# A fused transformer block on one core: k projections by depth block, and the q weights two steps later

## The chip, the core and the metric

The kernel runs on one core of a Trainium2 chip. A core has a matrix engine (TensorE; PE in the profile, its weight loads PEld), a vector engine (VectorE, DVE), a scalar engine for functions of one argument (ScalarE, ACT), a general engine (GpSimd, POOL) and SyncE (SP), which here issues the DMAs. Each engine works through its own queue in order and waits for others through semaphores. TensorE writes its products to PSUM, which has eight banks of 128 x 512 fp32 here; DVE and ACT read them there. The metric is the time on the device in microseconds (us), median of several runs.

## The reference

One token sequence of 2048 rows and 512 columns goes through a linear-attention block and a gated feed-forward block, both behind a layer norm whose scale and shift come from a condition vector:

```python
mod = (_silu(c) @ w_mod).reshape(c.shape[0], 6, 1, -1)
sa, ca, ga, sb, cb, gb = (mod[:, 0], mod[:, 1], mod[:, 2], mod[:, 3], mod[:, 4], mod[:, 5])
h = _layernorm(x, axis=-1) * (1 + ca) + sa
x = x + ga * _A_ref(h, A_wqkv, A_wo)
h = _layernorm(x, axis=-1) * (1 + cb) + sb
x = x + gb * _B_ref(h, B_w_gate, B_w_up, B_w_down)
```

`_A_ref` has 32 heads of 16 columns: q, k, v are projections of h, phi(t) is t + 1 above zero and exp(t) below, plus 1e-6; kv is the sum over all tokens of phi(k) times v, z the sum of phi(k); the output is (phi(q) kv) / (phi(q) z + 1e-6), times wo. `_B_ref` is ((h w_gate) * (h w_up)) w_down with 1376 inner columns.

## The kernel before

Everything is fp32. A matrix product is made of three passes on numbers cut into a high and a low part: high x high, high x low, low x high (`product`, L191 to L198). A *split* is one ACT copy for the high part (L183) and one DVE subtraction for the low part (L184).

**Tiles.** The tokens are 4 chunks of 4 tiles of 128 rows, 16 token tiles in all, numbered i = 4 ch + j. The 512 columns are 4 depth blocks of 128. `Norm` holds a chunk: `stats` (two DVE operations for a tile, L225 and L226), `rstd_of` (a DVE addition at L233, then a power on POOL at L234), `nmr_of` (L237, DVE), `xhat` (the normalised tile, one ACT operation, L243), `transpose` (L250, four 128 x 128 transposes for a depth block, which needs the normalised tiles of the whole chunk) and `modulated` (L262 onward: ACT applies scale and shift to a transposed block, giving f; its high part is a DVE cast, L270, or a second ACT operation, L272; its low part a DVE subtraction, L273).

**The start.** While the inputs arrive, TensorE is kept busy by `keep_on(n)` (L143), n matmuls whose result nobody reads. Chunk 0 is normalised and transposed, the modulation vectors ca and sa are summed up on DVE (L159, L161) and turned into columns by TensorE: `mod_col` (L166) writes four columns into one bank, and `col_out` (L171) is one DVE operation that reads all four. Then the four k weights are split and the four depth blocks of chunk 0 modulated, and `product2` (L206 to L208) makes the k projections of token tiles 0 and 1 together, depth block by depth block. The projections of tiles 2 and 3 follow through `proj`, a whole tile at a time.

**The loop.** Over the 16 token tiles the kernel sums up T = xhat^T phi(k) in four banks (`t_tile`, L327 to L329, 12 matmuls for a tile), from which kv is made later with the v weights. Step i makes the projection of tile i + 2 ahead of its use; splits the normalised tile (`k_split_x`) and phi of tile i + 1 (`k_split`, kh on ACT at L318 and kl on DVE at L319); does `k_phi` of tile i + 2 (Relu at L291 and Exp at L292 on ACT, then L295 on DVE); adds to z (L310, L312); and runs `t_tile(i)`. In steps 0 and 1 of each chunk it *turns* the next chunk: `t_tile` of two column blocks, transposes of two depth blocks, their modulation, the other two column blocks. The next-but-one chunk's statistics are done in steps 2 and 3 of a chunk, followed in step 3 by rstd, nmr and the first two normalised tiles; the other two come in step 0 of the next chunk. So the turn of chunk 2 is in steps 4 and 5.

The table `q_at` says in which steps a q projection of chunk 0 is made (12 matmuls, then phi on ACT and DVE), and the table `extra` what is done at the end of a step: the splits of the q and v weights, and the loads and sums of the other modulation vectors.

Each engine's order is the order of the text (the schedule is manual). PSUM has two pools of four banks, `acc_bank` and `bank`; a bank is given out again when the last instruction that uses it has been issued in that order.

After the loop come the kv matrix, the attention output by token tiles (L614) and the feed-forward block, whose products (L838 and L914 to L916) take most of the span.

Of the kernel before, what the change touches and what calls it, by code (L numbers as in the profile page):

```python
# [8 lines left out]
F32 = mybir.dt.float32  # L9
F32R = mybir.dt.float32r  # L10
AF = mybir.ActivationFunctionType
ALU = mybir.AluOpType
AX = mybir.AxisListType

P = 128
# [7 lines left out]
def tile_adaln_block(  # L23
# [12 lines left out]
    nc = tc.nc  # L36
# [3 lines left out]
    KD = D // P  # L40
    NJ = 4
    CH = NJ * P
    NCH = S // CH
# [16 lines left out]
    consts = pool("consts", 1)  # L60
# [5 lines left out]
    def f32(ap):  # L66
        return ap.bitcast(F32)
# [3 lines left out]
    def T(p, tag, shape=(P, D), dt=F32, bufs=None):  # L71
        cnt[0] += 1
        return p.tile(list(shape), dt, tag="t" if p is tiles else tag, name=f"{tag}_{cnt[0]}", bufs=bufs)

    def B(tag, shape=(P, D), dt=F32):

        return T(tiles, tag, shape, dt)

    def acc_bank():
        return T(ps_acc, "acc")  # L80

    def bank():
        return T(ps_w, "bank")
# [6 lines left out]
    ones = consts.tile([P, P], F32, name="ones")  # L90
# [28 lines left out]
    def load_qkv(n):  # L119
        return [load(wqkv_v[k, :, n * D:(n + 1) * D], "raw") for k in range(KD)]  # L120
# [6 lines left out]
    raw_k = load_qkv(1)  # L127
    xts.append(load_x(1))
    raw_q = load_qkv(0)
    raw_v = load_qkv(2)  # L130
# [10 lines left out]
    def keep_on(n):  # L141
        for _ in range(n):
            nc.tensor.matmul(ps_idle, idle[:, :P], idle, start=True, stop=True)  # L143
# [19 lines left out]
    def mod_col(acc, ps):  # L163

        for b in range(KD):
            nc.tensor.matmul(ps[:, b:b + 1], acc[:, b * P:(b + 1) * P], ones[:, 0:1], start=True, stop=True)  # L166
        return ps

    def col_out(v, ps, add):
        t = consts.tile([P, KD], F32, name=f"col{v}")  # L170
        nc.vector.tensor_scalar(t, ps[:, :KD], add, None, op0=ALU.add)  # L171
        return t
# [9 lines left out]
    def split(src, h, l, low=None):  # L182
        nc.scalar.activation(h, src, AF.Copy)  # L183
        (low or nc.vector).tensor_tensor(l, src, f32(h), op=ALU.subtract)  # L184

    def split_raw(raw, shape=(P, D), low=None):
        h = B("w", shape, F32R)
        l = B("w", shape, F32R)
        split(raw, h[:raw.shape[0]], l[:raw.shape[0]], low)
        return h, l  # L190
# [6 lines left out]
            nc.tensor.matmul(ps, ah, bl, start=False, stop=False)  # L197
            nc.tensor.matmul(ps, al, bh, start=False, stop=i == n - 1)  # L198

    def product2(pss, pairs):  # L200

        n = len(pairs[0])
        for i in range(n):
            for ps, p in zip(pss, pairs):
                (ah, al), (bh, bl) = p[i]
                nc.tensor.matmul(ps, ah, bh, start=i == 0, stop=False)  # L206
                nc.tensor.matmul(ps, ah, bl, start=False, stop=False)
                nc.tensor.matmul(ps, al, bh, start=False, stop=i == n - 1)  # L208

    def cut(pair, a, b):  # L210
        return pair[0][:, a:b], pair[1][:, a:b]


    class Norm:
# [25 lines left out]
        def xhat(self, *js):  # L240
            for j in js:
                self.n[j] = B("n")
                nc.scalar.activation(self.n[j], self.tiles[j], AF.Identity,  # L243
                                     scale=self.rstd[:, j:j + 1], bias=self.nmr[:, j:j + 1])

        def transpose(self, *ks):
            for k in ks:
# [29 lines left out]
    NT = NCH * NJ  # L277
    norm = [Norm(xts[0])]
    wk, wq, wv = [], [], []
    kx, phk, phq, q_ps = {}, {}, {}, {}  # L280

    def proj(i, w, of=bank):

        ch, j = divmod(i, NJ)
        ps = of()
        product(ps, [(cut(norm[ch].t[k], j * P, (j + 1) * P), w[k]) for k in range(KD)])
        return ps

    def phi_a(ps, t):

        nc.scalar.activation(t, ps, AF.Relu, scale=-1.0)  # L291
        nc.scalar.activation(t, t, AF.Exp, scale=-1.0)  # L292
# [4 lines left out]
    def k_split_x(i):  # L297
        ch, j = divmod(i, NJ)
        kx[i] = [B("xh", dt=F32R), B("xl", dt=F32R)]
        split(norm[ch].n[j], *kx[i])  # L300

    def k_phi(i, ps):
        phi = B("phi")
        phi_a(ps, phi)
        phi_b(ps, phi)
        phk[i] = phi
# [8 lines left out]
    def k_split(i):  # L315
        h, l = B("kh", dt=F32R), B("kl", dt=F32R)
        phi = phk[i]
        nc.scalar.activation(h, phi, AF.Identity, bias=eps_phi)  # L318
        nc.vector.scalar_tensor_tensor(l, phi, EPS_PHI, f32(h), op0=ALU.add, op1=ALU.subtract)  # L319
        kx[i] += [h, l]  # L320

    def t_tile(i, *ks):
        xh, xl, kh, kl = kx[i]
        first, last = i == 0, i == NT - 1
        for k in ks:
            a, b = k * P, (k + 1) * P
            nc.tensor.matmul(tacc[k], xh[:, a:b], kh, start=first, stop=False)  # L327
            nc.tensor.matmul(tacc[k], xl[:, a:b], kh, start=False, stop=False)  # L328
            nc.tensor.matmul(tacc[k], xh[:, a:b], kl, start=False, stop=last)  # L329
# [11 lines left out]
    n0 = norm[0]  # L341
    acc_ca, acc_sa = B("f"), B("f")
# [20 lines left out]
    mod_acc(acc_sa, raw_sa, [0, 1, 2, 3])  # L363
    ca = col_out(1, ps_ca, 1.0)
    keep_on(4)
    ps_sa = mod_col(acc_sa, acc_bank())
    keep_on(9)
    wk.append(split_raw(raw_k[0]))
    sa = col_out(0, ps_sa, 0.0)
    nx = Norm(xts[1])  # L370
    nx.stats(0)
    n0.modulated(ca, sa, 0, cast=nc.vector)
    wk.append(split_raw(raw_k[1]))
    n0.modulated(ca, sa, 1, cast=nc.vector)
    wk.append(split_raw(raw_k[2]))
    n0.modulated(ca, sa, 2)
    nx.stats(1)
    wk.append(split_raw(raw_k[3]))
    n0.modulated(ca, sa, 3)
    ps0, ps1 = acc_bank(), acc_bank()  # L380
    product2((ps0, ps1), [[(cut(n0.t[k], j * P, (j + 1) * P), wk[k]) for k in range(KD)] for j in range(2)])
    nx.stats(2, 3)
    nx.rstd_of()
    k_split_x(0)
    k_phi(0, ps0)
    nx.nmr_of()
    k_phi(1, ps1)
    k_split(0)
    nx.xhat(0, 1)

    tacc = [acc_bank() for _ in range(KD)]
    rows, cols = {}, {}
# [4 lines left out]
    def mod_load(*vs):  # L397
        raw_m.update({v: load_mod(v) for v in vs})

    def mod_part(v, *ks):  # L400
        if 0 in ks:
            accs[v] = B("f")
        mod_acc(accs[v], raw_m[v], ks)

    extra = {0: lambda: (wq.extend(split_raw(r) for r in raw_q[0:1]),),
             1: lambda: (wq.extend(split_raw(r) for r in raw_q[1:2]),),
             2: lambda: (wq.extend(split_raw(r) for r in raw_q[2:4]),),
             4: lambda: (wv.extend(split_raw(r) for r in raw_v[0:1]),),
             5: lambda: (wv.extend(split_raw(r) for r in raw_v[1:2]),),
             6: lambda: (wv.extend(split_raw(r) for r in raw_v[2:3]), mod_load(2),),  # L410
             7: lambda: (wv.extend(split_raw(r) for r in raw_v[3:4]),),
             8: lambda: (mod_part(2, 0, 1), mod_load(3)),
             9: lambda: (mod_part(2, 2, 3), mod_load(4)),
# [2 lines left out]
             12: lambda: (raw_o.extend(load(wo_v[k], "raw") for k in range(KD)), mod_part(4, 2, 3), cols.update({3: col_out(3, mod_col(accs[3], bank()), 0.0)})),  # L416
             13: lambda: (mod_part(5, 0, 1, 2), cols.update({4: col_out(4, mod_col(accs[4], bank()), 1.0)})),
             14: lambda: (mod_part(5, 3), wo_s.extend(split_raw(x) for x in raw_o)), 15: lambda: rows.update({5: mod_row(5, accs[5])})}
    q_at = {3: 0, 4: 1, 6: 2, 7: 3}
    ahead = {2: proj(2, wk)}  # L420
    for i in range(NT):
        ch, j = divmod(i, NJ)
        more = ch + 1 < NCH
        if i == 0:
            ahead[3] = proj(3, wk)
        elif i > 1:
            ahead[i + 2] = proj(i + 2, wk) if i + 2 < NT else proj(i + 6 - NT, wq)
        if i in q_at:
            qps = proj(q_at[i], wq)
        if more and j == 0:  # L430
            nx.xhat(2)
        if i + 1 < NT:
            k_split_x(i + 1)
        if more and j == 0:
            nx.xhat(3)
        if i + 1 < NT:
            k_split(i + 1)
        if more and j < 2:
            t_tile(i, 0, 1)
            nx.transpose(2 * j, 2 * j + 1)  # L440
            nx.modulated(ca, sa, 2 * j, 2 * j + 1, cast=nc.vector)
            norm[ch + 1:] = [nx]
        if ch + 2 < NCH and j == 2:
            nx2 = Norm(xts[ch + 2])
            nx2.stats(0, 1)
        if ch + 2 < NCH and j == 3:
            nx = nx2
            nx.stats(2, 3)
            nx.rstd_of()
            nx.nmr_of()  # L450
            nx.xhat(0, 1)
        if i + 2 < NT:
            k_phi(i + 2, ahead.pop(i + 2))
        else:
            q_a(i + 6 - NT, ahead.pop(i + 2))
            q_b(i + 6 - NT)
        if i in q_at:
            q_a(q_at[i], qps)
            q_b(q_at[i])
        if i + 1 < NT:  # L460
            z_add(i + 1)
        if i == NT - 1:
            zps = bank()
            nc.tensor.matmul(zps, ones, zacc, start=True, stop=True)
            zb = consts.tile([P, D], F32, name="zb")
            nc.scalar.activation(zb, zps, AF.Identity, bias=eps_z)
        t_tile(i, *range(2 if more and j < 2 else 0, KD))
        if i in extra:
            extra[i]()
    ga, gb, sb, cb = rows[2], rows[5], cols[3], cols[4]  # L470
# [60 lines left out]
    ps = proj(6, wq)  # L531
# [12 lines left out]
    for g in range(KD):  # L544
        a, b = g * P, (g + 1) * P
# [4 lines left out]
    ps = proj(8, wq)  # L550
# [9 lines left out]
    ps = proj(9, wq)  # L560
# [460 lines left out]
    ps = proj(11, wq)  # L1021
# [176 lines left out]
```

## Time and profile before

| | |
|---|---|
| median of 3 runs | 569.85 us (569.65 to 570.39) |
| the profiled execution, its time | 570.02 us |
| its span in the profile | 568.3 us |
| instructions | 7356 |
| DVE, ACT, POOL busy | 373.1, 279.8, 186.2 us |
| moved by DMA | 59.34 MB |

The span runs from the first to the last recorded instruction; the execution's time is a little longer. A row of the time line gives the start, the duration, the engine, the line and operation, the output and input tiles, and in brackets how long the engine had been idle before it and what released it. Rows joined to one ("x8") give the first start and the stretch up to the last end. An instruction's listed duration can reach past the start of the next on its engine, since their parts overlap; where work follows work, the distance from start to start tells what an instruction costs. For TensorE this distance is best read from the weight loads (PEld), one before each matmul. DVE's 9 tenths of busy time in a slice mean that it has hardly a gap there; these stretches lie in the first tenth of the span:

```text
DVE  7876868868768876759767777745554434344445
ACT  3785857546456546445865545534333333334110
```

### The profile page before, as it was taken

To read this page: it belongs to the slowest core of one execution; us is meant where nothing else is said; L and a number is where in the kernel's file an instruction comes from. 1 tells how busy PE (TensorE), PEld (TensorE's weight loads), DVE (VectorE), ACT (ScalarE), POOL (GpSimd) and SP (SyncE) were. 2 spreads that over 40 slices of the span, in tenths; PEclk is the share of its full clock that TensorE was granted. 3 is DMA by queue.
4 is the path that set the end of the run, shared out by engine and by line. 5 is a ranking of instruction groups with operands and counts; after the bars stand their busy time and mean duration, and the time that the engine had idled before them with its cause. 6 is when DMAs were issued, how large, how long until landed. Compare 5 with 4: busy or idle time off the path is not lost.

```text
span 568.3 us, 7356 instructions
## 1 busy us (share of the span) xinstructions
PE 560.3 (99%) x2575; PEld 458.8 (81%) x2575; DVE 373.1 (66%) x614; ACT 279.8 (49%) x500; POOL 186.2 (33%) x191
## 2 busy tenths in 40 slices
PE   8999999999999999999989999999999999999997
PEld 6778888888888878878878888787888888888886
DVE  7876868868768876759767777745554434344445
ACT  3785857546456546445865545534333333334110
POOL 2000000000011300000579666665667446556200
PEclk9999999999999999999999999999999999999999
DMA  8900223302301000804208553599336012200004
GB/s 289 374 3 2 74 75 110 114 0 62 93 0 47 29 1 37 260 0 149 57 2 277 180 190 104 202 348 330 115 111 178 26 57 55 57 19 2 0 1 148
DMA packets 50309, 59.34 MB, mean 104 GB/s; under 512 B 6432, under 2 KB 27168, under 8 KB 50272
## 3 DMA queue, kind: packets, MB, share of 16 engines
q1 hardware_dynamic: 50272, 58.87, 32.1%
q8 instruction: 20, 0.33, 0.2%
q14 instruction: 17, 0.14, 0.1%
HBM read 43.12 MB, written 15.73 MB: 104 GB/s over the span
## 4 chain that ended last, share of the span: by engine, by line
PE 89%; DMA 3%; issue 2%; POOL 1%; DVE 1%; ACT 1%; SPq 1%; POOLq 0%; ACTq 0%
PE bank L838 28%; PE acc L914 6%; PE acc L915 6%; PE acc L916 6%; PE acc L614 6%; PE bank L198 5%; PE bank L196 5%; PE bank L197 5%; PE acc L329 3%; PE acc L327 3%; PE acc L328 3%; PE bank L693 2%; PE bank L691 2%; PE bank L692 2%; PE bank L250 2%
## 5 line engine op out<-in xcount | busy, mean ns | idle before, releaser
L838 PE MATMUL bank<-h,w 128*128 128x512 f32 (+1 forms) x798 | 185.5, 390 | 1.8 <-ACT bank L843 1.2
L838 PEld LDWEIGHTS bank<-h,w 128*128 128x128 f32 (+1 forms) x798 | 148.2, 186 | 35.3 <-ACT bank L843 1.7
L843 ACT ACTIVATE bank<-bank 128x512 f32<-128x512 f32 (+1 forms) x38 | 22.1, 583 | 144.8 <-PE bank L838 144.8
L678 DVE TENSOR_TENSOR x<-acc,x 128x512 f32<-128x512 f32 (+1 forms) x73 | 49.1, 684 | 49.0 <-PE acc L916 48.2
L824 POOL TENSOR_TENSOR w<-raw,w 128x256 fp32r<-128x256 f32 (+3 forms) x38 | 42.4, 1117 | 106.4 <-ACT w L817 86.4
L184 POOL TENSOR_TENSOR w<-raw,w 128x512 fp32r<-128x512 f32 (+1 forms) x25 | 34.9, 1399 | 116.0 <-DVE mv L226 87.6
L914 PE MATMUL acc<-w,kh 128*128 128x512 f32 (+2 forms) x154 | 59.6, 387 | 0.0
L915 PE MATMUL acc<-w,kh 128*128 128x512 f32 (+2 forms) x154 | 59.6, 387 | 0.0
L916 PE MATMUL acc<-w,kl 128*128 128x512 f32 (+2 forms) x154 | 59.5, 386 | 0.0
L234 POOL TENSOR_TENSOR rstd<-ve,half 128x4 f32<-128x4 f32 (+1 forms) x9 | 9.4, 1044 | 126.0 <-DVE ve L233 124.5
L184 DVE TENSOR_TENSOR kl<-u,kh 128x512 fp32r<-128x512 f32 (+1 forms) x38 | 26.8, 746 | 33.1 <-ACT kh L183 31.2
L824 POOL TENSOR_TENSOR w<-t,w 128x512 fp32r<-128x512 f32 (+1 forms) x38 | 48.4, 1293 | 0.0
L196 PE MATMUL bank<-w,h 128*128 128x512 f32 x112 | 45.0, 402 | 0.0
L198 PE MATMUL bank<-w,h 128*128 128x512 f32 x112 | 43.9, 392 | 0.0
L197 PE MATMUL bank<-w,h 128*128 128x512 f32 x112 | 43.6, 389 | 0.0
L614 PE MATMUL acc<-w,xh 128*128 128x512 f32 x120 | 38.1, 399 | 0.0
L914 PEld LDWEIGHTS acc<-w,kh 128*128 128x128 f32 (+1 forms) x154 | 28.9, 188 | 6.0
L916 PEld LDWEIGHTS acc<-w,kl 128*128 128x128 f32 (+1 forms) x154 | 28.9, 188 | 5.9
L915 PEld LDWEIGHTS acc<-w,kh 128*128 128x128 f32 (+1 forms) x154 | 28.9, 188 | 5.9
L893 DVE TENSOR_TENSOR u<-bank,u 128x512 f32<-128x512 f32 (+1 forms) x19 | 13.1, 690 | 30.0 <-PE bank L838 30.0
L243 ACT ACTIVATE n<-x,nmr,rstd 128x512 f32<-128x512 f32 x32 | 24.1, 804 | 17.2 <-DVE nmr L237 15.9
L262 ACT ACTIVATE f<-bank,col,col 128x512 f32<-128x512 f32 x28 | 20.7, 775 | 14.5 <-PE bank L250 12.4
(177 smaller groups left out, 1105.1 us busy)
## 6 DMA issues: line engine op xcount, KB each, us to landing
raw<-in_w_mod_dram SPq DMA_DIRECT2D x24, 256.0 KB, 3.7
raw<-in_B_w_down_dram SPq DMA_DIRECT2D x20, 256.0 KB, 2.9
raw<-in_B_w_gate_dram SPq DMA_DIRECT2D x36, 128.0 KB, 3.7
raw<-in_B_w_up_dram SPq DMA_DIRECT2D x36, 128.0 KB, 3.6
x<-in_A_x_dram SPq DMA_DIRECT2D x16, 256.0 KB, 5.4
kept<-f SPq DMA_DIRECT2D x16, 256.0 KB, 2.0
f<-kept SPq DMA_DIRECT2D x16, 256.0 KB, 4.8
side_s<-h SPq DMA_DIRECT2D x16, 256.0 KB, 2.6
```

What stands on the lines that cost most here:

```text
L184: (low or nc.vector).tensor_tensor(l, src, f32(h), op=ALU.subtract)
L196: nc.tensor.matmul(ps, ah, bh, start=i == 0, stop=False)
L197: nc.tensor.matmul(ps, ah, bl, start=False, stop=False)
L198: nc.tensor.matmul(ps, al, bh, start=False, stop=i == n - 1)
L243: nc.scalar.activation(self.n[j], self.tiles[j], AF.Identity, scale=self.rstd[:, j:j + 1], bias=self.nmr[:, j:j + 1])
L614: nc.tensor.matmul(yps[i], x, y, start=False, stop=k == KD - 1 and x is al, skip_group_check=True)
L678: nc.vector.tensor_tensor(xt[:, a:b], dn[j][:, a:b], xt[:, a:b], op=ALU.add)
L824: sub = lambda out, x, y: (on or nc.gpsimd).tensor_tensor(out, x, f32(y), op=ALU.subtract)
L838: mm = lambda x, y, **kw: nc.tensor.matmul(ps, x[:, k], y, skip_group_check=True, **kw)
L914: nc.tensor.matmul(ps, hh[:, a:b], dh[:n, c:d], start=i == 0, stop=False)
L915: nc.tensor.matmul(ps, hh[:, a:b], dl[:n, c:d], start=False, stop=False)
L916: nc.tensor.matmul(ps, hl[:, a:b], dh[:n, c:d], start=False, stop=i == len(hs) - 1)
```

## The change

Four things are changed, all of them in the first 100 us.

- The sa columns: the first is written into a bank of its own and read alone (`sa_out(0)`); the three others share a second bank and are read one by one behind block 0. Nine `keep_on` matmuls behind them become two.
- The k projections of tiles 0 to 3 are made depth block by depth block for all four tiles (`k_block`), in four banks; for blocks 2 and 3 the order is by tile. `product2` goes. All four blocks of chunk 0 take their high part by a DVE cast (before, blocks 2 and 3 took it from ACT).
- Chunk 1 is normalised in halves: statistics, rstd and nmr for its tiles 0 and 1, then statistics and rstd for tiles 2 and 3, which DVE normalises itself (`xhat_on`). Its turn moves from steps 0 and 1 to steps 1 and 2; in step 2 it stands ahead of `t_tile(2)`, and that ahead of the projection of tile 4.
- The splits of the q weights move from steps 0, 1, 2 to steps 2, 3, 4, the q projections from steps 3, 4, 6, 7 to steps 5, 6, 7, 8, and the splits of the v weights from 4, 5, 6, 7 to 5, 6, 7.

```diff
+        def xhat_on(self, engine, *js):
+            for j in js:
+                self.n[j] = B("n")
+                engine.tensor_scalar(self.n[j], self.tiles[j], self.mv[:, j, 0:1], self.rstd[:, j:j + 1],
+                                     op0=ALU.subtract, op1=ALU.mult)
...
-    ps_sa = mod_col(acc_sa, acc_bank())
-    keep_on(9)
-    wk.append(split_raw(raw_k[0]))
-    sa = col_out(0, ps_sa, 0.0)
+    ps_sa = [acc_bank()]
+    ps_sa += [acc_bank()] * (KD - 1)
+    sa = consts.tile([P, KD], F32, name="col0")
+
+    def sa_block(b):
+        nc.tensor.matmul(ps_sa[b][:, b:b + 1], acc_sa[:, b * P:(b + 1) * P], ones[:, 0:1], start=True, stop=True)
+
+    def sa_out(b):
+        nc.vector.tensor_scalar(sa[:, b:b + 1], ps_sa[b][:, b:b + 1], 0.0, None, op0=ALU.add)
+
+    def block_in(b):
+        n0.modulated(ca, sa, b, cast=nc.vector)
+
+    def w_in(b):
+        wk.append(split_raw(raw_k[b]))
+
+    for b in range(KD):
+        sa_block(b)
+    keep_on(2)
+    k_ps = [acc_bank(), acc_bank(), bank(), bank()]
+
+    def k_block(b, *js):
+        for j in js:
+            (hh, hl), (wh, wl) = cut(n0.t[b], j * P, (j + 1) * P), wk[b]
+            nc.tensor.matmul(k_ps[j], hh, wh, start=b == 0, stop=False)
+            nc.tensor.matmul(k_ps[j], hh, wl, start=False, stop=False)
+            nc.tensor.matmul(k_ps[j], hl, wh, start=False, stop=b == KD - 1)
+
+    sa_out(0)
+    w_in(0)
+    block_in(0)
+    for b in range(1, KD):
+        sa_out(b)
+    w_in(1)
+    block_in(1)
+    k_block(0, 0, 1, 2, 3)
     nx = Norm(xts[1])
+    w_in(2)
+    block_in(2)
     nx.stats(0)
-    n0.modulated(ca, sa, 0, cast=nc.vector)
-    wk.append(split_raw(raw_k[1]))
-    n0.modulated(ca, sa, 1, cast=nc.vector)
-    wk.append(split_raw(raw_k[2]))
-    n0.modulated(ca, sa, 2)
+    k_block(1, 0, 1, 2, 3)
+    w_in(3)
+    block_in(3)
     nx.stats(1)
-    wk.append(split_raw(raw_k[3]))
-    n0.modulated(ca, sa, 3)
-    ps0, ps1 = acc_bank(), acc_bank()
-    product2((ps0, ps1), [[(cut(n0.t[k], j * P, (j + 1) * P), wk[k]) for k in range(KD)] for j in range(2)])
+    nx.rstd_of(0, 2)
+    k_split_x(0)
+    k_block(2, 0)
+    k_block(3, 0)
+    k_phi(0, k_ps[0])
+    nx.nmr_of(0, 2)
+    nx.xhat(0, 1)
     nx.stats(2, 3)
-    nx.rstd_of()
-    k_split_x(0)
-    k_phi(0, ps0)
-    nx.nmr_of()
-    k_phi(1, ps1)
+    nx.rstd_of(2, 4)
     k_split(0)
-    nx.xhat(0, 1)
+    k_block(2, 1)
+    k_block(3, 1)
+    k_split_x(1)
+    k_phi(1, k_ps[1])
+    nx.xhat_on(nc.vector, 2)
+    k_split(1)
+    nx.xhat_on(nc.vector, 3)
+    k_block(2, 2)
+    k_block(3, 2)
+    k_block(2, 3)
+    k_block(3, 3)
...
-    extra = {0: lambda: (wq.extend(split_raw(r) for r in raw_q[0:1]),),
-             1: lambda: (wq.extend(split_raw(r) for r in raw_q[1:2]),),
-             2: lambda: (wq.extend(split_raw(r) for r in raw_q[2:4]),),
-             4: lambda: (wv.extend(split_raw(r) for r in raw_v[0:1]),),
-             5: lambda: (wv.extend(split_raw(r) for r in raw_v[1:2]),),
-             6: lambda: (wv.extend(split_raw(r) for r in raw_v[2:3]), mod_load(2),),
+    extra = {2: lambda: (wq.extend(split_raw(r) for r in raw_q[0:1]),),
+             3: lambda: (wq.extend(split_raw(r) for r in raw_q[1:2]),),
+             4: lambda: (wq.extend(split_raw(r) for r in raw_q[2:4]),),
+             5: lambda: (wv.extend(split_raw(r) for r in raw_v[0:1]),),
+             6: lambda: (wv.extend(split_raw(r) for r in raw_v[1:3]), mod_load(2),),
              7: lambda: (wv.extend(split_raw(r) for r in raw_v[3:4]),),
...
-    q_at = {3: 0, 4: 1, 6: 2, 7: 3}
-    ahead = {2: proj(2, wk)}
+    q_at = {5: 0, 6: 1, 7: 2, 8: 3}
+    ahead = {2: k_ps[2], 3: k_ps[3]}
+    turn_at = {4 * ch + j: (ch + 1, 2 * j, 2 * j + 1) for ch in range(1, NCH - 1) for j in range(2)}
+    turn_at.update({1: (1, 0, 1), 2: (1, 2, 3)})
     for i in range(NT):
         ch, j = divmod(i, NJ)
-        more = ch + 1 < NCH
-        if i == 0:
-            ahead[3] = proj(3, wk)
-        elif i > 1:
+        done = 0
+        if i > 2:
             ahead[i + 2] = proj(i + 2, wk) if i + 2 < NT else proj(i + 6 - NT, wq)
         if i in q_at:
             qps = proj(q_at[i], wq)
-        if more and j == 0:
+        def turn_x():
+            to, *ks = turn_at[i]
+            nx.transpose(*ks)
+            nx.modulated(ca, sa, *ks, cast=nc.vector)
+            norm[to:] = [nx]
+
+        fresh = i > 0 and ch + 1 < NCH and j == 0
+        if i == 2:
+            turn_x()
+        if fresh:
             nx.xhat(2)
-        if i + 1 < NT:
+        if 0 < i < NT - 1:
             k_split_x(i + 1)
-        if more and j == 0:
+        if fresh:
             nx.xhat(3)
-        if i + 1 < NT:
+        if 0 < i < NT - 1:
             k_split(i + 1)
-        if more and j < 2:
+        if i in turn_at and i != 2:
             t_tile(i, 0, 1)
-            nx.transpose(2 * j, 2 * j + 1)
-            nx.modulated(ca, sa, 2 * j, 2 * j + 1, cast=nc.vector)
-            norm[ch + 1:] = [nx]
+            done = 2
+            turn_x()
+        if i == 2:
+            t_tile(i, *range(KD))
+            done = KD
+            ahead[i + 2] = proj(i + 2, wk)
...
-        t_tile(i, *range(2 if more and j < 2 else 0, KD))
+        t_tile(i, *range(done, KD))
```

More of the change, by code (lines that the diff above doesn't have):

```diff
@@ L198, in product @@
             nc.tensor.matmul(ps, al, bh, start=False, stop=i == n - 1)
[L200 to L208, printed above, removed]
     def cut(pair, a, b):
```

## The prediction

> **What bounds the kernel now.** I read the page first, then the list of what the weight loads waited for, then the time lines of PE, DVE and ACT over the first 60 us, since the change ends there.
>
> ```profile
> span 568.3 us, 7356 instructions
> ...
> PE 560.3 (99%) x2575; PEld 458.8 (81%) x2575; DVE 373.1 (66%) x614; ACT 279.8 (49%) x500; POOL 186.2 (33%) x191
> ```
>
> ```profile
> PEld bank L838 <- ACT bank L843: 1.7, 1, 1.7
> ...
> PEld acc L208 <- DVE h L273: 0.8, 2, 0.4
> PEld bank L198 <- DVE h L273: 0.7, 2, 0.4
> ```
>
> TensorE is busy for 99% of the span, and once products run its waits are small: the longest is 1.7 us. The number of products is not changed. So the time moves only by how early the useful stream starts and by waits put into it or taken out, and what is gained or lost up to the point where both orders have issued the same products is carried to the end.
>
> ```profile
> 14.94 0.97 PEld L166 LDWEIGHTS acc<-ones,f 128*128 128x128 f32 x8 [0.33 <-DVE f L161]
> 15.82 1.94 PEld L143 LDWEIGHTS acc<-w 128*128 128x128 f32 x9
> 16.03 0.16 DVE L171 TENSOR_SCALAR col<-acc 128x4 f32<-128x4 f32 x1 [0.47 <-PE acc L166]
> 16.23 0.78 ACT L262 ACTIVATE f<-bank,col,col 128x512 f32<-128x512 f32 x1 [1.96 <-DVE col L171]
> 17.80 0.19 PEld L206 LDWEIGHTS acc<-w,h 128*128 128x128 f32 x1
> 18.34 0.19 PEld L208 LDWEIGHTS acc<-w,h 128*128 128x128 f32 x1
> 23.23 0.50 PE L208 MATMUL acc<-w,h 128*128 128x512 f32 x1
> 23.76 0.60 ACT L291 ACTIVATE phi<-acc 128x512 f32<-128x512 f32 x1 [1.33 <-PE acc L208]
> 24.93 0.58 ACT L291 ACTIVATE phi<-acc 128x512 f32<-128x512 f32 x1
> 29.49 0.19 PEld L327 LDWEIGHTS acc<-kh,xh 128*128 128x128 f32 x1
> 34.66 0.68 DVE L295 SCALAR_TENSOR_TENSOR phi<-bank,phi 128x512 f32<-128x512 f32 x1
> 35.26 0.68 DVE L310 TENSOR_TENSOR z<-phi,phi 128x512 f32<-128x512 f32 x1
> ...
> 42.81 0.19 PEld L196 LDWEIGHTS bank<-w,h 128*128 128x128 f32 x1
> 49.73 0.17 DVE L233 TENSOR_SCALAR ve<-mv 128x4 f32<-128x4 f32 x1
> 51.12 0.16 DVE L237 SCALAR_TENSOR_TENSOR nmr<-mv,rstd 128x4 f32<-128x4 f32 x1 [1.21 <-POOL rstd L234]
> 53.88 0.58 ACT L291 ACTIVATE h<-bank 128x512 f32<-128x512 f32 x1
> 55.03 0.80 ACT L243 ACTIVATE n<-x,nmr,rstd 128x512 f32<-128x512 f32 x1
> 56.26 0.80 ACT L243 ACTIVATE n<-x,nmr,rstd 128x512 f32<-128x512 f32 x1
> 57.77 1.03 PEld L250 LDWEIGHTS bank<-ident,n 128*128 128x128 f32 x8
> ```
>
> These rows are merged in order of time; left is the start, then the duration. Two places matter. At the start, the one DVE read of the four sa columns waits for all eight passes of L166 (16.03), and products begin at 17.80, behind nine idle-filling matmuls of L143. Later, at i=4, the transposes of chunk 2 load at 57.77, 0.71 us after the last normalised tile that they read (56.26 + 0.80 = 57.06). That slack is small, and it is there because TensorE has the q products of tiles 0 and 1 to do at i=3 and i=4.
>
> **Units.** From the load at 42.81 (product of tile 5) to 57.77 TensorE issues 66 matmuls: four projections, t_tile(3) and half of t_tile(4). One takes 14.96/66 = 0.227 us. DVE starts a tensor operation 0.60 us after the one before (34.66 to 35.26), though each is listed with 0.68. The other steps follow, from start to start, and first eight transposes from the chain of waits:
>
> ```profile
> 58.16 0.87 PE bank L250 x8
> ```
>
> ```profile
> 28.97 0.62 ACT L183 ACTIVATE xh<-n 128x512 fp32r<-128x512 f32 x1
> 29.49 0.80 ACT L243 ACTIVATE n<-x,nmr,rstd 128x512 f32<-128x512 f32 x1
> 30.20 0.71 ACT L318 ACTIVATE kh<-phi,eps_phi 128x512 fp32r<-128x512 f32 x1
> ...
> 33.60 0.42 DVE L270 CAST h<-f 128x512 fp32r<-128x512 f32 x1
> 34.05 0.69 DVE L273 TENSOR_TENSOR h<-f,h 128x512 fp32r<-128x512 f32 x1
> ...
> 42.80 0.69 DVE L225 BATCH_NORM_STATS2 st<-x 128x6 f32<-128x512 f32 x1
> ...
> 43.62 0.66 DVE L225 BATCH_NORM_STATS2 st<-x 128x6 f32<-128x512 f32 x1
> ```
>
> Copy 0.52 and normalise 0.71 on ACT; cast 0.45 and statistics with their aggregation 0.82 on DVE. One phi (Relu, Exp) is 24.93 - 23.76 = 1.17 on ACT.
>
> **The first column.** With a bank of its own it is ready after two of eight passes: 6 x 0.97/8 = 0.73 us earlier, read at 15.30, and ACT's block 0 starts at 15.50 instead of 16.23 and ends 16.28. DVE does the low part of the first k weight at 15.40 (before, it lay in the wait for the columns), the cast at 16.32, the low half from 16.77 to 17.46. Seven idle-filling matmuls go at no cost: the two that stay end near 16.3, ahead of the cast. The third matmul of the first product loads at 17.51, against 18.34: 0.8 us earlier. The other three reads (0.1 us each) stand on DVE behind block 0, and ACT's block 1 behind them, at 17.8; no matmul waits for that.
>
> **Four token tiles per block.** A block now feeds 12 matmuls, 2.7 us, where DVE needs 0.60 + 0.45 + 0.60 = 1.65 us for a weight and a block, new casts included, or 2.47 with a statistics. So the two waits at L208 shrink to one of 0.3: DVE, without a gap from 19.05 on, ends block 3's low half at 23.9. But tile 0 is finished behind 30 matmuls instead of 21: the stream, counted back from the third matmul, starts at 17.05; the last load would be at 17.05 + 29 x 0.227 = 23.65 and waits until 23.9. With 0.5 us of drain (23.23) the first phi starts at 24.45, where it started at 23.76. The 18 matmuls of the other tiles run to 28.2; before, the same 48 were done at 29.49: 1.3 us ahead here.
>
> **The first t_tiles.** TensorE now goes straight to t_tile(0), which needs kh and kl of tile 0. ACT does in its order: phi to 25.7; two normalisations at 26.6 and 27.3 (they follow nmr, which follows phi's DVE half, 25.8 + 0.6); kh from 28.0 to 28.7. TensorE waits from 28.2 to 28.75, and 0.27 more for kl (to 29.45). Tile 1 goes on in the same way: copy 28.6, phi 29.15, DVE half 30.5, kh 31.2 to 31.9. That adds 0.1 at the bank of t_tile(0)'s last column block and 0.35 at t_tile(1). New waits in sum: 1.25 us. They buy out the two at L198 (0.7): with t_tile(2) ahead of it, tile 4's product finds chunk 1's blocks ready. It ends at 42.15 by this chain (t_tile(0) ends at 31.9, then 36 matmuls, the 0.35, and two sets of eight transposes at 0.9). The same products were done at 42.81: **0.65 us gained so far**.
>
> The two tiles normalised on VectorE have no row of their form. The nearest are the modulation's operation below and the tensor operation of 0.68:
>
> ```profile
> 12.04 0.48 DVE L159 TENSOR_SCALAR f<-raw,sc 128x512 f32<-128x512 f32 x1
> ```
>
> I take 0.5, the row nearest in form. Both fall into gaps in which DVE waits for kh or phi (0.4 to 0.5 us each), so by the other end it is 0.2 us more at most. The second rstd falls into POOL's idle time.
>
> **The q weights later.** This decides. No DMA is moved (the raw q weights are loaded at the start, and the next loads stay at i=6), but the q products leave i=3, 4, 6, 7 for 5 to 8. TensorE then reaches chunk 2's transposes after proj(5), t_tile(3), proj(6) and half of t_tile(4): 42 x 0.227 = 9.55 us after 42.15, at 51.7. Of the 6.05 us by which this is earlier than 57.77, 5.45 are the two q products.
>
> Are the tiles there? DVE's half of tile 2's phi starts at 33.1 (kh of tile 1 leaves ACT at 31.8, then 1.27 of phi), against 34.66. From it to the end of the statistics DVE has 17 tensor operations, 4 casts and 4 statistics, each with its input there in time: 17 x 0.60 + 4 x 0.45 + 4 x 0.82 = 15.3, so ve comes at 48.45. (By this count the order before, with 18, 2 and 4, takes 15.0; the rows show 49.73 - 34.66 = 15.07.) The rstd takes 51.12 - 49.73 = 1.39: nmr at 49.85. Then ACT took 57.06 - 51.12 = 5.94 to the last tile; a q phi goes out of it (55.03 - 53.88 = 1.15) and the copy of the second q weight comes in (0.52): 5.3. The last tile is there at 55.2. **TensorE waits 3.5 us**, and all its later products, the q products too, are queued behind these transposes.
>
> **Sum.** A gain of 0.65 and a wait of 3.5 make +2.9 (or: 55.25 for the transposes, plus 5.45 of products still owed, less 57.77). Later turns give nothing back: at i=8 all four q products lie ahead of chunk 3's transposes, as they did, and TensorE stays the bound. The profiled execution took 570.02 us, with a span of 568.3, so this one would take 572.9; the median of the runs is 0.17 lower, hence **572.8 us**.
>
> **Rivals.** (a) *DVE closes its gaps.* My chain has 2.6 us of DVE waits between 15 and 33 us, for blocks (0.3, 0.3), phi (0.5, 0.5) and kh (0.5, 0.4, 0.1). With none, ve is at 45.85, the transposes at 52.6, the sum 0.3: 570.1. Against it: all of these inputs come from ACT in a fixed order. (b) *The turn is not late*: if nmr is there by 46.4 (51.7 - 5.3), i=4 has no wait and the gain of 0.65 stays, 569.2; with the kh waits gone too it is 1.9, 567.9. For it speaks that ACT idles in places, against it that DVE's work alone ends later. (c) *The first column is not earlier*, if its read still waits for all passes: 0.73 more, 573.5. (d) *The wait slows TensorE behind it.*
>
> ```profile
> 6.00 1.97 PEld L143 LDWEIGHTS acc<-w 128*128 128x128 f32 x5
> ...
> 292.18 2.59 PEld L838 LDWEIGHTS bank<-h,w 128*128 128x128 f32 x12 [1.66 <-ACT bank L843]
> ```
>
> At the start of the run matmuls go every 0.4 us until about 8 us. If 3.5 us without work bring this back for as long, 15 matmuls lose 0.17 each: +2.6, 575.4. After 1.66 us of waiting (292.18) twelve loads take 0.22 each, so that wait did not.
>
> [...]
>
> **How the numbers follow.** Forecast 0.70, (a) 0.09, (b) 0.07, (c) 0.06, (d) 0.08. A measurement here tells some 0.2%, 1.1 us, from no change, so same is 568.7 to 571.0. Slower is the forecast, (c) and (d), less 0.04 for a wait that falls far short: 0.80. Same is (a), that 0.04 and a little of (b): 0.14; faster is the rest, 0.06. The range goes from (a), 570.1, to just inside (d), 575.0.
>
> **What would show it.** Right: a wait of 3 to 4 us at L250 near 51.7 us, released by ACT's n; the first phi at 24.5; short waits at L327 to L329 near 28 us. Wrong: no wait over 1 us at L250 between 45 and 60 us, or ve before 46.5, or DVE work with gaps between 33 and 48 us, which would be a wait that my chain misses.

## The result

| | before | change |
|---|---|---|
| median | 570.18 us (6 runs, 569.65 to 570.82) | 573.02 us (6 runs, 571.59 to 574.66) |
| ratio to before | | 1.0048, 95% interval 1.0037 to 1.0060 |
| the profiled execution's span | 568.3 us | 572.9 us |
| its mean granted clock | 0.999 | 0.994 |

The change makes the kernel 2.8 us slower; 2.9 were forecast. The profiled execution, at 574.66, is the slowest of the six, and its page shows something that the page of before doesn't have:

```profile
span 572.9 us, 7349 instructions
...
PE 561.2 (98%) x2568; PEld 458.9 (80%) x2568; DVE 375.3 (66%) x622; ACT 276.7 (48%) x496; POOL 186.3 (33%) x192
...
PEclk9998899999999999999999999999999999999999
```

In the clock's row the fourth and fifth slices (43 to 72 us) are below full. The list of waits of the weight loads names the new waits (total, times, longest):

```profile
PEld bank L246 <- ACT n L233: 3.2, 2, 2.1
...
PEld acc L323 <- ACT kh L314: 0.9, 2, 0.6
PEld acc L325 <- DVE kl L315: 0.9, 2, 0.4
```

L246 is the line of the chunk transposes (L250 before); L323 and L325 are `t_tile` (L327, L329). No product L198 stands in the list any more. Rows chosen from the time lines of PEld, ACT and DVE of the changed kernel, merged, from the start to the late turn:

```profile
12.15 2.33 DVE L161 SCALAR_TENSOR_TENSOR f<-raw,sc,f 128x512 f32<-128x512 f32 x3
14.96 0.16 DVE L370 TENSOR_SCALAR col<-acc 128x1 f32<-128x1 f32 x1 [0.40 <-PE acc L367]
17.17 0.19 PEld L388 LDWEIGHTS acc<-w,h 128*128 128x128 f32 x1 [0.36 <-DVE h L269]
23.92 0.60 ACT L287 ACTIVATE phi<-acc 128x512 f32<-128x512 f32 x1 [3.02 <-PE acc L388]
28.20 0.19 PEld L323 LDWEIGHTS acc<-kh,xh 128*128 128x128 f32 x1 [0.65 <-ACT kh L314]
28.93 0.19 PEld L325 LDWEIGHTS acc<-kl,xh 128*128 128x128 f32 x1 [0.43 <-DVE kl L315]
...
41.48 0.19 PEld L196 LDWEIGHTS bank<-w,h 128*128 128x128 f32 x1
47.95 0.17 DVE L223 TENSOR_SCALAR ve<-mv 128x4 f32<-128x4 f32 x1
49.33 0.16 DVE L227 SCALAR_TENSOR_TENSOR nmr<-mv,rstd 128x4 f32<-128x4 f32 x1 [1.21 <-POOL rstd L224]
51.00 0.37 PEld L246 LDWEIGHTS bank<-ident,n 128*128 128x128 f32 x2
53.47 0.14 PEld L246 LDWEIGHTS bank<-ident,n 128*128 128x128 f32 x1 [2.09 <-ACT n L233]
53.84 0.80 ACT L233 ACTIVATE n<-x,nmr,rstd 128x512 f32<-128x512 f32 x1
54.69 0.93 PEld L246 LDWEIGHTS bank<-ident,n 128*128 128x128 f32 x5 [1.09 <-ACT n L233]
55.60 0.34 PEld L323 LDWEIGHTS acc<-kh,xh 128*128 128x128 f32 x1
```

Two rows of the kernel before, for comparison:

```profile
12.56 2.33 DVE L161 SCALAR_TENSOR_TENSOR f<-raw,sc,f 128x512 f32<-128x512 f32 x3
58.76 0.19 PEld L327 LDWEIGHTS acc<-kh,xh 128*128 128x128 f32 x1
```

The input data came 0.41 us earlier in this execution than in that of before: the sum over sa ends at 12.15 + 2.33 = 14.48, against 12.56 + 2.33 = 14.89 there. All that follows is shifted by it, so it is taken off in what is said of steps. TensorE is at the transposes at 51.0, does those of the first two tiles, waits 2.09 us for the third tile and 1.09 for the fourth. The second half of `t_tile(4)` loads at 55.60. Before, it loaded right behind the transposes, at 58.76. With the 5.45 us of q products still owed and the shift of 0.41, the turn is 55.60 + 5.45 + 0.41 - 58.76 = 2.7 us late.

What comes behind is the second loss. The stages of the changed kernel: start and end, length, then the busy time and instructions of PE, PEld, DVE, ACT and POOL, and at the end granted clock, DMA share and GB/s:

```profile
50.00:52.00 2.00, 1.61 (x9) 1.09 (x7) 0.00 (x0) 1.97 (x4) 0.00 (x0) 1.00 0.00 0
52.00:54.00 2.00, 0.33 (x1) 0.14 (x1) 1.78 (x3) 2.00 (x5) 0.00 (x0) 0.99 0.00 0
54.00:56.00 2.00, 1.31 (x6) 1.31 (x7) 1.41 (x3) 1.98 (x3) 0.00 (x0) 0.50 0.00 0
56.00:58.00 2.00, 2.00 (x7) 1.52 (x6) 1.84 (x4) 1.91 (x4) 0.00 (x0) 0.50 0.00 0
58.00:60.00 2.00, 2.00 (x6) 1.60 (x5) 2.00 (x4) 2.00 (x4) 0.00 (x0) 0.50 0.20 31
60.00:62.00 2.00, 2.00 (x8) 1.59 (x7) 1.91 (x4) 0.16 (x1) 0.00 (x0) 0.81 0.94 307
```

Between 54 and 60 us TensorE runs at half its clock (0.50 in these three stages). Its loads then follow each other by 0.43 us, and it does 13 matmuls from 55.60 to 60.88, which at 0.227 take 2.95 us: 2.3 us lost. So the spans' difference of 4.6 is made up: -0.41 from the data, +2.7 from the turn, +2.3 from the clock. Some 0.4 of the 2.7 is the clock as well: the last five transposes take 0.93 us here, and 0.53 in e2_q_late_alone below, where it was still full.

The low stretch here lasts from 53.96, by the mean of 0.99 in the 52 to 54 stage, to 60.76, by the 0.81 in the last one: some 6.8 us. In three other traces below (e1, e2, e5) it is half of that, 3.4 us: e5's stages stand below, e2's of 2 us from 54 on have means of 0.98, 0.50 and 0.66, and e1's of 4 us from 8 on 0.99 and 0.59. The clock fell within the second of the two waits, when the loads had waited 2.4 us in sum (2.09 and, from 53.61 on, 0.35). In e2 and e5 it fell 0.65 and 0.4 us behind the second wait, with 2.4 and 3.2 us waited in sum; in e1, 1.5 us behind a single wait of 2.6. Behind a wait of 2.21 us in e6's trace it stayed at 1.00. What sets the moment of the fall and the length of the low stretch isn't shown.

### The profile page after: what moved, and what is told of

It reads as the page before. It is cut to its first block, busy times and chain, and to the rows that moved or that the text cites. A ratio compares the mean times of both kernels' runs of the same rounds, so it can differ in the third digit from the quotient of the medians.

```text
span 572.9 us, 7349 instructions
## 1 busy us (share of the span) xinstructions
PE 561.2 (98%) x2568; PEld 458.9 (80%) x2568; DVE 375.3 (66%) x622; ACT 276.7 (48%) x496; POOL 186.3 (33%) x192
## 4 chain that ended last, share of the span: by engine, by line
PE 85%; DVE 4%; ACT 4%; issue 2%; DMA 2%; POOL 2%; SPq 0%; POOLq 0%; DVEq 0%
PE bank L886 27%; PE acc L963 6%; PE acc L962 6%; PE acc L964 6%; PE acc L662 6%; PE bank L196 4%; PE bank L197 4%; PE bank L198 4%; PE bank L741 2%; PE bank L739 2%; PE bank L740 2%; PE acc L325 2%; PE acc L323 2%; PE acc L324 2%; PE bank L246 2%
## 5 line engine op out<-in xcount | busy, mean ns | idle before, releaser
L184 DVE TENSOR_TENSOR kl<-u,kh 128x512 fp32r<-128x512 f32 (+1 forms) x38 | 27.3, 757 | 33.1 <-ACT kh L183 31.2
L196 PE MATMUL bank<-w,h 128*128 128x512 f32 x104 | 42.2, 406 | 0.0
L197 PE MATMUL bank<-w,h 128*128 128x512 f32 x104 | 41.0, 394 | 0.0
L198 PE MATMUL bank<-w,h 128*128 128x512 f32 x104 | 40.9, 394 | 0.0
L233 ACT ACTIVATE n<-x,nmr,rstd 128x512 f32<-128x512 f32 x30 | 22.6, 804 | 17.8 <-DVE nmr L227 17.8
```

## The experiments

All ratios are against the kernel before on the same chip. e1 to e4 ran on one chip, where its median was 570.87 us; e5 to e8 and then e9 and e10 ran on another, where it was 570.65 and 570.48. Where the text says that a run was at full clock, its mean granted clock was 0.999 or 1.000. The kernel before was below that in 4 of its 76 runs, all in the last group.

**e1_q_back: the q tables of before in the changed kernel.** (The splits of the v weights, in the lines left out, go back with them.)

```diff
-    extra = {2: lambda: (wq.extend(split_raw(r) for r in raw_q[0:1]),),
-             3: lambda: (wq.extend(split_raw(r) for r in raw_q[1:2]),),
-             4: lambda: (wq.extend(split_raw(r) for r in raw_q[2:4]),),
+    extra = {0: lambda: (wq.extend(split_raw(r) for r in raw_q[0:1]),),
+             1: lambda: (wq.extend(split_raw(r) for r in raw_q[1:2]),),
+             2: lambda: (wq.extend(split_raw(r) for r in raw_q[2:4]),),
...
-    q_at = {5: 0, 6: 1, 7: 2, 8: 3}
+    q_at = {3: 0, 4: 1, 6: 2, 7: 3}
```

> The change with the two tables of the q weights as before: splits at the end of steps 0, 1, 2, q projections in steps 3, 4, 6, 7. Theory (the q products are what covered the making of chunk 2's normalised tiles): no wait above 0.3 us at the transposes of chunk 2; the other parts come to -0.1 to -0.6 us, so 569.6 to 570.1. Rival (the loss comes from the new order of the start, the late first phi and the waits at the first t_tiles): it stays above 571.5.

Measured: 569.31 us, ratio 0.9975 (0.9966 to 0.9985). The wait at chunk 2's transposes is gone: they load as eight, without an idle time in front.

```profile
43.88 0.19 PEld L198 LDWEIGHTS bank<-w,h 128*128 128x128 f32 x1 [0.43 <-DVE h L269]
48.48 0.19 PEld L197 LDWEIGHTS bank<-w,h 128*128 128x128 f32 x1 [0.17 <-DVE w L184]
59.04 1.02 PEld L246 LDWEIGHTS bank<-ident,n 128*128 128x128 f32 x8
```

So the q tables turn a gain into a loss, and the other three parts of the change are a gain: 1.4 us, more than the 0.1 to 0.6 that I had expected. The trace that was kept is of the slowest of the twelve runs, 571.17 us, the only one below full clock. There the clock fell at the start, behind a wait of 2.6 us for the first chunk's tiles, and not at chunk 2's turn (a stage, then two rows of the time line):

```profile
12.00:14.00 2.00, 2.00 (x9) 1.52 (x8) 1.93 (x4) 0.51 (x1) 0.00 (x0) 0.50 1.04 384
...
12.93 2.33 DVE L161 SCALAR_TENSOR_TENSOR f<-raw,sc,f 128x512 f32<-128x512 f32 x3
17.17 0.16 DVE L370 TENSOR_SCALAR col<-acc 128x1 f32<-128x1 f32 x1 [0.99 <-PE acc L367]
```

The first column is read 17.17 - 15.26 = 1.91 us behind the sum over sa, where the changed kernel's trace has 14.96 - 14.48 = 0.48. Without these 1.43 us chunk 2's transposes come 59.04 - 15.26 - 1.43 = 42.35 us behind the sum, against 57.77 - 14.89 = 42.88 before. By this estimate 0.5 us are gained up to there, as expected; where the other 0.9 come from stays open.

**e2_q_late_alone: only the q tables, in the kernel before** (the same edit the other way round).

> The kernel before with only the two tables of the q weights of the change. Theory: ve comes 1.8 us earlier (three splits fewer ahead of it on DVE), TensorE 5.45 + 0.8 us earlier, so it waits some 2.5 us at chunk 2's transposes and the sum is +2.0 to +2.3 us: 572.2 to 572.5 where the clock holds, up to 2.6 us more in runs in which it halves behind the wait. Rival (start order): no change, 569.9 to 570.5.

Measured: 572.61 us, ratio 1.0034 (1.0022 to 1.0046), +1.9 us. At full clock (four of eight runs) the median is 572.06, just below the 572.2 to 572.5 expected, but only 1.2 over this chip's median of before, less than the 2.4 us of waits in its trace; why, stays open. The late turn comes from the tables alone, with no part of the new start: the loads of the transposes wait in the same two pieces.

```profile
54.04 0.14 PEld L250 LDWEIGHTS bank<-ident,n 128*128 128x128 f32 x1 [1.32 <-ACT n L243]
55.27 0.53 PEld L250 LDWEIGHTS bank<-ident,n 128*128 128x128 f32 x5 [1.09 <-ACT n L243]
```

**e3_fill_wait: 14 idle-filling matmuls ahead of the late transposes.**

```diff
-            nx.transpose(*ks)
+            nx.transpose(*ks, fill=14 if i == 4 else 0)
...
                 ps = turn_bank[0]()
+                for _ in range(fill if k == ks[0] else 0):
+                    nc.tensor.matmul(ps, idle[:, :P], idle, start=True, stop=True)
```

> The change with 14 idle-filling matmuls into the bank of the first transposes at step 4, ahead of them: 14 x 0.227 = 3.2 us, inside the wait. Theory (the halved clock behind the wait is a cost of its own, present in some runs): granted clock 1.00 in every run, times within 1.2 us of each other as those of before are, median 571.4 to 572.4. Rival (the clock costs nothing, the wait is all): as the change, 573.0 with a scatter of 3 us.

Measured: 571.92 us, ratio 1.0025 (1.0016 to 1.0034). The stages of its trace:

```profile
50.00:55.00 5.00, 5.00 (x26) 4.09 (x25) 2.49 (x4) 4.97 (x9) 0.00 (x0) 1.00 0.00 0
55.00:60.00 5.00, 5.00 (x26) 4.25 (x26) 4.43 (x8) 4.97 (x9) 0.00 (x0) 1.00 0.36 113
```

TensorE is kept busy through the wait and the clock stays at 1.00. Ten of its twelve runs are at full clock, with a median of 571.87; the two others (0.997 and 0.996; 573.10 and 572.80) have no trace, and where their clock fell isn't known. On the same chip e1 has 569.30 in its runs at full clock, so the late turn by itself costs 2.6 us. The changed kernel without the fill was not run on this chip.

**e5_change_again: the changed kernel once more.**

> The changed kernel itself, on the chip of the next three runs. Theory (a late turn of 2.0 to 2.7 us, and a halved clock behind it in part of the runs): 2.0 to 2.9 us over before in the median, runs with granted clock 0.999 or 1.000 near +2.0, runs with 0.994 to 0.997 up to 2.6 us above those. Rival (the scatter is not tied to the clock): times do not fall with the clock.

Measured: 573.06 us, ratio 1.0038 (1.0025 to 1.0050). One of the five runs has a clock of 0.999, with 571.47 us; the other four (0.996, 0.997) take 572.72 to 573.50, median 573.08, 1.6 more. This time the low stretch is half as long, as the stages show:

```profile
54.00:56.00 2.00, 1.10 (x7) 0.97 (x7) 1.43 (x3) 2.00 (x4) 0.00 (x0) 0.85 0.00 0
56.00:58.00 2.00, 2.00 (x7) 1.52 (x6) 1.86 (x5) 1.97 (x5) 0.00 (x0) 0.50 0.00 0
58.00:60.00 2.00, 2.00 (x9) 1.60 (x8) 2.00 (x4) 2.00 (x5) 0.00 (x0) 0.80 0.18 30
60.00:62.00 2.00, 2.00 (x10) 1.67 (x9) 2.00 (x4) 0.24 (x1) 0.00 (x0) 1.00 0.96 313
```

Together with the six runs of the result, 8 of 11 runs of the changed kernel have a clock below 0.998. In e2, where the wait is shorter, it is 4 of 8, and their median is 573.23 against 572.06 for the others. A run's mean doesn't tell where in it the clock fell: the traces of the result, of e5 and of e2 have it at chunk 2's turn, that of e1 at the start.

**e6_tiles_ahead: the last two tiles of chunk 2 normalised at once with the first two.**

```diff
-        fresh = i > 0 and ch + 1 < NCH and j == 0
+        fresh = i > 4 and ch + 1 < NCH and j == 0
...
-            nx.xhat(0, 1)
+            nx.xhat(*(range(NJ) if i == 3 else (0, 1)))
```

> The change, with the last two normalised tiles of chunk 2 made on ACT right behind the first two, in step 3: ahead of one phi (1.17), one weight copy (0.52) and one tile copy (0.52). Theory (the chain on ACT behind nmr sets the wait): the wait at chunk 2's transposes falls by 2.2 us to about 1, and the time by 2.2 us or more against the change, so between -0.3 and +0.7 us to before; the clock stays at 1.000. Rival (what counts is when DVE ends the statistics, or the displaced phi is late in turn): it gains less than 1 us on the change.

Measured: 571.60 us, ratio 1.0025 (1.0015 to 1.0036). That is 1.5 us less than the change's median in e5 (573.06), between the 2.2 of the theory and the rival's 1, and it comes mostly from the clock: 9 of its 12 runs are at full clock, with a median of 571.37, and the change's one such run in e5 has 571.47. The waits at the transposes did fall by 2.2 us, from 3.2 to 1.0:

```profile
51.80 0.14 PEld L246 LDWEIGHTS bank<-ident,n 128*128 128x128 f32 x1 [0.43 <-ACT n L233]
52.51 0.53 PEld L246 LDWEIGHTS bank<-ident,n 128*128 128x128 f32 x5 [0.57 <-ACT n L233]
...
60.79 0.19 PEld L197 LDWEIGHTS bank<-w,h 128*128 128x128 f32 x1 [2.21 <-DVE w L184]
```

The chain on ACT was named rightly, and the 2.2 us were lost again 8 us later: the first q product, now reached sooner, waits 2.21 us for the low part of a q weight, whose split the change had moved to the end of step 4. The two tables make two things late, and only the first had shown.

**e4_column_alone: the first column's bank, in the kernel before.**

```diff
-    ps_sa = mod_col(acc_sa, acc_bank())
-    keep_on(9)
-    wk.append(split_raw(raw_k[0]))
-    sa = col_out(0, ps_sa, 0.0)
-    nx = Norm(xts[1])
-    nx.stats(0)
-    n0.modulated(ca, sa, 0, cast=nc.vector)
+    ps_sa = [acc_bank()]
+    ps_sa += [acc_bank()] * (KD - 1)
...
+    keep_on(2)
...
+    sa_out(0)
+    wk.append(split_raw(raw_k[0]))
+    n0.modulated(ca, sa, 0, cast=nc.vector)
+    for b in range(1, KD):
+        sa_out(b)
+    nx = Norm(xts[1])
+    nx.stats(0)
```

> The kernel before with only the first sa column in a bank of its own, two idle-filling matmuls behind it, and the statistics of the next chunk's first tile behind block 0. The prediction's step taken alone: products start 0.7 us earlier and the end is 0.7 us earlier, 569.4. Rival (with two token tiles for a block VectorE sets the pace, and its work of this stretch has only lost the cover of the column's wait): block 1 is late by 1.0 to 1.2 us on TensorE, and the end is where it was or 0.3 us later, 570.0 to 570.6.

Measured: 570.48 us, ratio 0.9995 (0.9985 to 1.0004): no change to be seen. The products start earlier and the second block is late, as the rival had it:

```profile
17.05 0.19 PEld L206 LDWEIGHTS acc<-w,h 128*128 128x128 f32 x1 [0.78 <-PE acc L143]
17.71 0.19 PEld L208 LDWEIGHTS acc<-w,h 128*128 128x128 f32 x1 [0.37 <-DVE h L273]
19.65 0.19 PEld L206 LDWEIGHTS acc<-w,h 128*128 128x128 f32 x1 [1.18 <-DVE h L270]
```

With two token tiles for a block TensorE needs 1.4 us a block, less than VectorE's 1.65. So the earlier column is worth nothing with two tiles; that it is worth something with four is argued, since no run takes it out of the change. (The stretches in which DVE is 9 tenths busy do not lie in the first tenth of the span, as the section on the profile says: its row has 7, 8, 7 and 6 there. That VectorE is the limit here is read from these waits for it.)

**e9_stats_behind: the statistics of chunk 1's first tile behind block 1, in the kernel before.**

```diff
-    nx = Norm(xts[1])
-    nx.stats(0)
     n0.modulated(ca, sa, 0, cast=nc.vector)
     wk.append(split_raw(raw_k[1]))
     n0.modulated(ca, sa, 1, cast=nc.vector)
+    nx = Norm(xts[1])
+    nx.stats(0)
```

> The kernel before with the statistics of chunk 1's first tile moved on VectorE from ahead of block 0's cast to behind block 1. Theory (on this machine they often wait for that tile's DMA, 0.85 us in one trace, and hold up block 0): 0.4 to 0.8 us less than before. Rival (VectorE's list of work is the bound, and a place in it is worth nothing): within 0.3 us of before.

Measured: 570.62 us, ratio 1.0001 (0.9992 to 1.0010). The theory fell: on this chip the order before has such a wait too (0.64 us in e8's trace), the trace of e9 doesn't, and nothing is gained. That makes it unlikely that the 0.85 us of e2's trace are what e1 gained beyond the expectation; on the chip of e1 and e2 the move was not run.

**e8_before_pool and e7_q_back_pool: the low parts of the q weights and of the fourth k weight on GpSimd,** in the kernel before and in e1.

```diff
-    wk.append(split_raw(raw_k[3]))
+    wk.append(split_raw(raw_k[3], low=nc.gpsimd))
...
-    extra = {0: lambda: (wq.extend(split_raw(r) for r in raw_q[0:1]),),
+    extra = {0: lambda: (wq.extend(split_raw(r, low=nc.gpsimd) for r in raw_q[0:1]),),
```

> The kernel before with the low parts of the four q weights and of the fourth k weight on GpSimd, nothing else. Theory (VectorE's list of work sets the products' waits in the first 40 us): the waits at L198 (0.7) and one at L208 (0.4) and L207 (0.2) go, -0.9 to -1.3 us to before. Rival (as above): no change.

> The change with the q tables of before, and the low parts of the four q weights and of the fourth k weight on GpSimd (1.4 us each there, idle then) in place of VectorE (0.6 each). Theory (VectorE's list of work sets the blocks of chunk 1 and of block 3): the waits left at L198 and L388 go (0.3 + 0.2 + 0.2 us), so 0.5 to 0.8 us less than with the q tables alone, 1.9 to 2.3 us less than before. Rival (GpSimd slows VectorE, or its rstd is late): no gain over the q tables alone, -1.4.

Measured: e8 571.89 us, ratio 1.0017 (1.0008 to 1.0026); e7 570.30 us, 0.9993 (0.9984 to 1.0002). By the ratios both are about 1 us slower than without the move (e7 against e1's 0.9975, each on its own chip). Rows of e8, POOL and DVE merged:

```profile
35.64 0.68 DVE L295 SCALAR_TENSOR_TENSOR phi<-bank,phi 128x512 f32<-128x512 f32 x1
35.89 1.29 POOL L184 TENSOR_TENSOR w<-raw,w 128x512 fp32r<-128x512 f32 x1 [8.45 <-ACT w L183]
36.24 1.49 DVE L310 TENSOR_TENSOR z<-phi,phi 128x512 f32<-128x512 f32 x1
37.66 0.68 DVE L184 TENSOR_TENSOR xl<-n,xh 128x512 fp32r<-128x512 f32 x1
...
40.17 1.31 POOL L184 TENSOR_TENSOR w<-raw,w 128x512 fp32r<-128x512 f32 x1 [2.98 <-ACT w L183]
40.37 1.65 DVE L273 TENSOR_TENSOR h<-f,h 128x512 fp32r<-128x512 f32 x1
```

Each subtraction on GpSimd takes its 0.60 us off DVE, but the DVE operation with both inputs in SBUF that begins while it runs lasts 1.49 or 1.65 instead of 0.68. The one with an input in PSUM (35.64) runs on undisturbed, with 0.68. The first ends at 36.24 + 1.49 = 37.73, 0.55 after GpSimd's end at 37.18. So it is with five such operations in the traces of e8 and e7: they last 1.49 to 1.79 us and end 0.54 to 0.56 after GpSimd, not much less than the 0.60 that one costs by itself. That looks as if each waited for GpSimd's end; no row shows the wait itself.

**e10_start_reordered: e1, with ACT's order between the first phi and the first t_tiles changed.** The edit changes VectorE's order too: nmr and the subtraction for tile 1's normalised x go ahead of the first phi, and kl of tile 0 ahead of the second rstd's addition.

```diff
     k_split_x(0)
     k_block(2, 0)
     k_block(3, 0)
+    k_split_x(1)
+    nx.nmr_of(0, 2)
+    k_block(2, 1)
+    k_block(3, 1)
     k_phi(0, k_ps[0])
-    nx.nmr_of(0, 2)
-    nx.xhat(0, 1)
+    nx.xhat(0)
     nx.stats(2, 3)
-    nx.rstd_of(2, 4)
     k_split(0)
-    k_block(2, 1)
-    k_block(3, 1)
-    k_split_x(1)
+    nx.rstd_of(2, 4)
     k_phi(1, k_ps[1])
+    nx.xhat(1)
     nx.xhat_on(nc.vector, 2)
     k_split(1)
-    nx.xhat_on(nc.vector, 3)
...
+    nx.xhat_on(nc.vector, 3)
```

> The change with the q tables of before, and ACT's order between the first phi and the first t_tiles changed: one normalised tile of chunk 1, kh of tile 0, the phi of tile 1, then the other normalised tile (before: both, then kh and the phi); the copy of tile 1's normalised x and the nmr go ahead of the first phi. Theory (kh of tile 0 and the phi of tile 1 set the waits at the first t_tiles): the waits at L323 and L325 near 28 to 33 us, 1.25 us in sum, shrink to 0.3, and the time is 2.0 to 2.6 us under before. Rival (the waits only move to the transposes of chunk 1 or to tile 4's product): as with the q tables alone, -1.0 to -1.9.

Measured: **567.37 us** (5 runs, 567.13 to 567.93), ratio 0.9941 (0.9927 to 0.9955), all five with a clock of 0.999 or 1.000. This version beats both kernels, before by 3.1 us, more than the 2.0 to 2.6 of the theory. Between the products of block 3 and the turn of chunk 2 one wait is left, and no product L198 waits:

```profile
28.82 0.19 PEld L325 LDWEIGHTS acc<-kl,xh 128*128 128x128 f32 x1 [0.50 <-DVE kl L315]
32.35 1.03 PEld L246 LDWEIGHTS bank<-ident,n 128*128 128x128 f32 x8
34.61 1.03 PEld L246 LDWEIGHTS bank<-ident,n 128*128 128x128 f32 x8
55.92 1.02 PEld L246 LDWEIGHTS bank<-ident,n 128*128 128x128 f32 x8
```

Its sum over sa ends at 14.77, so chunk 2's transposes come 41.15 us behind it, against 42.88 before: 1.7 us. From there to the end of the span it takes 509.8 us, against 510.5. That 0.7 us is one wait of before in the feed-forward block, which e10's trace lacks:

```profile
PEld bank L838 <- DVE u L893: 0.7, 1, 0.7
```

It is no merit of the edit: of the changed kernel's two traces the first has it (0.8) and e5's doesn't, so it comes and goes between executions of one kernel.

## Why the prediction was right

**The late turn: right, and over-priced.** The time line follows the forecast chain step for step, each counted from the end of the sum over sa: the first product's third matmul 2.69 us behind it (forecast 17.51 - 14.89 = 2.62), the first phi 9.44 (9.56), ve 33.47 (33.56), nmr 34.85 (34.96), the last tile's end 40.16 (40.31). The wait was 3.2 us for a forecast of 3.5. e1 and e2 show that the q tables make it, e6 that ACT's chain sets its length. At full clock it costs 2.6 us (e3 against e1), near the wait less some 0.4 us by which TensorE comes earlier when the q splits are not on VectorE's list (next paragraph). Rival (a), that DVE would close its gaps, did not come: they are where they were forecast, for phi, kh and blocks.

**The start: the sign right, the gain too small.** I gave 0.65 us to everything but the q tables; e1 measures 1.4. The waits at the first t_tiles are there with nearly the sizes named (0.65 and 0.43 idle at 28.20 and 28.93, for 0.55 and 0.27). The step "it ends at 42.15 by this chain ... 0.65 us gained" is nearly right in the changed kernel: the next product loads at 41.48, 27.0 us behind the sum over sa, where 27.3 was forecast and before has 27.9, so 0.9 is gained. Of this e1 keeps about 0.5 to the turn, since the q splits are back in VectorE's list and the waits at L198 and L197 with them (43.88 and 48.48). The rest of its 1.4 us lies outside the stretch that the prediction counted, and stays open.

**The clock: the step that failed.** The forecast took the sum without a halved clock and gave rival (d) a chance of 0.08. The measured ground for so low a chance is that 1.66 us of waiting had done nothing; the rest of it was my estimate. A low clock came in 8 of 11 runs, in the two with a trace behind 2.4 and 3.2 us of waiting in two pieces, the longer of 2.09. The price of 2.6 us given there doesn't follow from its own words either: matmuls 0.4 us apart for 3.5 us are 9 and not 15, and lose 1.5 us. Measured were 2.3, or 2.7 with the transposes, in the profiled execution, whose low stretch is 6.8 us long, and 1.2 to 1.6 in the medians of runs (e2, e5).

So the total came out right with three terms of which two were off: -0.65 + 3.5 + 0 was said, and -1.4 + 2.6 + about 1.4 was measured. That the errors nearly cancel is luck. At full clock the changed kernel's three runs took 571.47, 571.59 and 572.53 us, all below the forecast of 572.8. Rivals (b) and (c) did not occur: the turn was late, and the first column was read at 14.96, 0.4 us behind the load of its passes.

## What to carry over

- Work that an engine could do at any time is the cover of whatever it stands in front of. Before it is moved, list the next thing on that engine that waits for others, and compare its due time with the engine's arrival without the cover; here 5.45 us of products went, and 0.71 us of slack stood against it.
- Shortening one wait shows the next: e6 took 2.2 us out of the turn and paid 2.2 us at the first q product. In a stage where VectorE works without a gap, a piece gained elsewhere is worth what VectorE's list allows (e4, e9), and a new order of the same work on ACT and VectorE can be worth more than a new engine (e10 against e7).
- A wait of some 3 us on TensorE can cost half as much again behind it, in some executions and not in others (1.2 and 1.6 us between the medians of e2 and e5, behind 2.4 and 3.2 of waiting); filling it with matmuls that nobody reads got that part back in ten of twelve runs (e3).

## What was not expected of the hardware

- TensorE's clock fell to 0.50 behind short waits: in the four traces with a fall, the loads had waited 2.4 to 3.2 us in sum before it, in one or two pieces of 2.6 us at most. It stayed low for 6.8 us in one trace and 3.4 in the three others, so the time of one kernel scatters over 3 us (571.47 to 574.66).
- A subtraction of 1.28 to 1.45 us on GpSimd lengthened one VectorE operation with two SBUF inputs by 0.8 to 1.1 us (1.49 to 1.79 in the traces of e8 and e7, against 0.68), more than the 0.60 us that it took off VectorE.
